# Unit 1's decay sums behind unit 0's state product, in a bank of its own, without zero products: a linear attention and a two-layer network on one core

## The chip, the cores and the metric

The kernel runs on one core of one Trainium2 chip. The metric is the device time of one execution in microseconds (us). The core's engines have these names: PE multiplies matrices (PEld is its loading of weights), DVE is VectorE, ACT is ScalarE, POOL is GpSimd, and SP only issues DMAs. Each engine works through its own list of instructions in order and waits on semaphores for the others.

## The reference

A recurrent attention with a decay for every row of its state, and behind it a network of two layers with a squared relu. B, H, S, D are 4, 8, 768, 48; the width H·D is 384 and the hidden width 2048.

```python
for t in range(S):
    state = alpha[:, :, t, :, None] * state + np.einsum('bhd,bhe->bhde', k[:, :, t], v[:, :, t])
    y[:, :, t] = np.einsum('bhd,bhde->bhe', q[:, :, t], state)
...
x = y.transpose(0, 2, 1, 3).reshape(B * S, H * D)
h = x @ w_in
r = np.maximum(h, 0.0)
out = (r * r) @ w_out
```

## The kernel before

**Units.** The sequence of each of the four batches is cut into three pieces of 256 tokens. A piece of one batch is a unit; units 0 to 3 are the first pieces of the four batches, 4 to 7 the second, 8 to 11 the third. The decays are handled as sums of logarithms within a unit (a product with a triangle of ones), so that a unit needs only products of matrices and one state of the unit before it in its batch.

**Steps of a unit g**, each an operation with a name in the program:

- `lda`, `ldk`, `ldq`, `ldv`: the loads of alpha, k, q and v, 384 KB each. Units 1 to 3 and unit 4's alpha are loaded through GpSimd's queue, in which the pieces of the two weights stand too (`win0` to `win3`, `wout0` to `wout3`); later units through SP's. `lda2` waits for `ldv1`, `ldk1` for `ldk0`.
- Decays: `pr` (product of the alphas of a pair of tokens), `ln` and `lm` (logarithms, on ScalarE), the sums on PE (`m1`, for units 2 and up `m1i`), then the exponentials on ScalarE, `ei`, `ea`, `ec`, and `lb` with `es`, the same for the first token of a pair; `bk` multiplies a part of them.
- `ekm` and `eqm` multiply keys and queries by these. `vc` copies the values to bf16. `tr` transposes keys and queries (on PE up to unit 2, by DMA on SP from unit 3 on) and `et` copies them out of PSUM.
- `p` (scores, on PE; for units 1 and up with the products for the state in the same operation), `mk` (the causal mask), `kv` (unit 0's state product), `sa`, `sc`, `sd` (state at the middle and at the end of the unit), `y` (attention's output), `xe` and `xf` (copies of it), `xt` and `xv` (its transpose).
- The network: `s1_g_u` (first layer, eight pairs of hidden tiles), `re` (relu), `sq` (square), `s2_g_j_s` (second layer, a quarter of the sum each), `oe` (copy out of PSUM), `out` (store).

**Order.** `TABLES` holds one list of these names for each engine, and that is the order in which an engine does them. `add` notes for every operation what it reads and writes, the PSUM banks among them, and `place` sets a wait for another engine only where an operation needs it. So moving a name in a list moves waits too.

**Banks.** `psWH` has three banks: W, H0 and H1. `psO` is one bank: the second layer's sums, and now and then a pair of the first layer. `state_banks` says in which banks a unit's state products stand. For unit 0 these were H0 and H1: H0 is read by `sa0`, H1 by `sc0`. Unit 1's sums `m11` are written to W and H0, so `m11` had to wait for `sa0`. The banks of the sums of units 0 and 1, and those of unit 0's state products:

```python
bank, keys = (psX, [("ps", "X", 0), ("ps", "X", 1)]) if g == 0 else (psWH, [("ps", "W"), ("ps", "H", 0)])
...
return (psH[0][:, 0:HD], psH[1][:, 0:HD]), [("ps", "H", 0), ("ps", "H", 1)]
```

**Zero products.** Entries such as `+512` in PE's list are products of a tile of zeros, 512 or 256 columns wide, which write to `psO` and are read by nobody. They stand only in the first 17 us, between PE's operations of units 0 and 1. Nothing is noted of what they write.

Line numbers below are those of the kernel before: L992 is the first layer, L1038 the second, L1000 and L1002 the relu on ScalarE and VectorE, L1010 and L1014 the square on VectorE and ScalarE, L579 the sums of a later unit, L545 to L551 those of unit 1, L590 and L592 its exponentials `ei` and `ea`, L570 `pr`, L573 `ln`, L614 `lb`, L637 and L636 the copy of the values on ScalarE and GpSimd, L646 `ekm`, L894 the mask, L941 `xv`, L877 the scores, L1086 the zero products, L657 the transposes by DMA.

Of the kernel before, what the change touches and what calls it, by code (L numbers as in the profile page):

```python
# [204 lines left out]

TABLES = {
    "act": """
        table ln0_0 ln1_0 ei0_0 xcaus ea0_0 ei1_0 ea1_0 ec1_0 et00_0 ec0_0 vc0 ln1 et01_0 et11_0 vc1 ei1 ea1 xe0
        ec1 et0_1 re0_0 sa1 re0_1 sq0_1 re0_3 xe1 re0_4 re0_5 lm2 ln2 re0_6 ei2 ea2 ec2 es2 re1_2 re1_3 sq0_6
        re1_4 et0_2 vc2 re1_6 sa2 sq1_6 sq1_3 ln3 lm3 ei3 ea3 ec3 es3 oe0_0 oe0_1 xf2 xe2 lm4 ln4 vc3 ei4 ea4  # L210
        ec4 re2_0 re2_1 es4 oe1_0 re2_2 re2_3 re2_4 ldk5 re2_5 ldq5 sa3 sq2_5 lm5 re2_7 ln5 re2_6 xe3 ei5 ea5
        ec5 xv3 es5 oe2_0 re3_0 oe2_1 lm6 re3_1 xe4 ln6 re3_4 re3_3 ei6 ea6 ec6 re3_6 sq3_5 re3_7 sq3_7 es6
        re4_0 re4_1 re4_2 re4_3 vc6 xe5 lm7 ln7 re4_7 oe3_1 re4_4 ei7 ea7 ec7 re4_6 sq4_6 es7 oe4_0 re5_0 re5_1
        lm8 ln8 xe6 re5_2 re5_3 ei8 ea8 re5_4 re5_5 es8 re5_6 re5_7 sq5_7 re6_0 re6_1 re6_2 oe5_0 vc8 xe7 lm9
        ln9 re6_5 re6_6 oe5_1 re6_7 ei9 ea9 es9 oe6_0 vc9 re7_0 lm10 re7_1 ln10 xe8 re7_3 ei10 ea10 re7_4 re7_5
        es10 re7_6 re7_7 oe7_0 re8_0 re8_1 re8_2 lm11 ln11 xe9 re8_3 re8_4 ei11 ea11 re8_5 re8_6 sq8_5 es11
        sq8_7 re9_0 oe8_0 vc11 re9_1 oe8_1 xe10 re9_3 re9_4 re9_5 re9_6 re9_7 re10_0 oe9_0 re10_1 re10_2 xe11
        oe9_1 re10_3 re10_4 re10_5 re10_6 re10_7 re11_0 oe10_0 re11_1 re11_2 re11_3 oe10_1 re11_4 re11_5 re11_6
        re11_7 oe11_0 oe11_10
    """,  # L220
    "dve": """
        zero zlinc zlstr zident zcaus zcaus1 zla0 zla1 zones zown zown0 zown1 zqk0 zqk1 zqk2 zlb0 zlb1 ekm0_0
        eqm0_0 ekm1_0 eqm1_0 et10_0 mk0_0 sa0 mk1_0 ekm1 eqm0_1 eqm1_1 xv0 et1_1 sc0 mk1_1 mk0_1 sc1 re0_2 xf1
        sq0_3 xv1 pr2 sq0_5 re0_7 re1_0 lb2 re1_1 ekm2 eqm0_2 eqm1_2 sq0_7 re1_5 et1_2 sq1_1 sq1_5 re1_7 mk1_2
        pr3 sc2 mk0_2 lb3 eqm1_3 eqm0_3 ekm3 xv2 pr4 sq1_7 bk4 lb4 ekm4 eqm1_4 eqm0_4 sq2_1 mk1_3 mk0_3 sc3
        oe1_1 sd3 sq2_7 sq2_6 xf3 lb5 ekm5 eqm1_5 eqm0_5 sa4 mk1_4 mk0_4 re3_2 pr6 sc4 sq3_1 xf4 sq3_3 re3_5
        sq3_6 lb6 ekm6 sa5 mk0_5 sc5 mk1_5 eqm0_6 eqm1_6 oe3_0 xf5 sq4_1 re4_5 pr7 sq4_3 sq4_7 sq4_5 bk7 lb7
        eqm0_7 sa6 eqm1_7 ekm7 sc6 sd6 mk0_6 mk1_6 pr8 oe4_1 xf6 sq5_3 bk8 lb8 ekm8 sq5_5 sq5_6 sa7 mk0_7 sc7
        mk1_7 eqm0_8 eqm1_8 sq6_1 re6_3 sd7 sq6_3 pr9 xf7 re6_4 sq6_5 sq6_6 sq6_7 bk9 lb9 ekm9 eqm0_9 eqm1_9
# [4 lines left out]
    """,  # L234
    "pe": """
        +512 +512 +512 +512 +512 +512 +512 +512 m10_0 m11_0 +512 +512 +256 +256 tr00_0 +512 +256 tr10_0 +512
        +256 +256 tr01_0 p0_0 tr11_0 kv0 +512 +512 +512 +256 +256 p1_0 m11 +512 +256 y0 +512 +512 +256 tr0_1 xt0
        tr1_1 s1_0_0 p0_1 s1_0_1 s1_0_3 s1_0_2 s1_0_4 y1 s1_0_5 xt1 s1_0_6 s1_0_7 s1_1_0 m1i2 s1_1_1 s1_1_2
        s1_1_3 s1_1_4 s1_1_5 tr0_2 s1_1_6 tr1_2 s2_0_0_0 s1_1_7 p0_2 s2_0_0_1 s2_0_0_2 s2_0_1_0 s2_0_1_1 m1i3
        s2_0_1_2 s2_0_0_3 s2_0_1_3 y2 s2_1_0_0 s2_1_0_1 xt2 s2_1_0_2 s1_2_0 s1_2_1 m1i4 s2_1_0_3 s1_2_2 s1_2_3  # L240
        s2_1_1_0 s1_2_4 s2_1_1_1 s1_2_5 p0_3 s2_1_1_2 s1_2_6 s1_2_7 s2_1_1_3 y3 m1i5 s2_2_0_0 s2_2_0_1 xt3
        s2_2_0_2 s2_2_0_3 s1_3_0 p0_4 s2_2_1_0 s2_2_1_1 s2_2_1_2 s2_2_1_3 s1_3_2 s1_3_1 y4 s1_3_4 s1_3_3 m1i6
        s1_3_6 s1_3_5 s2_3_0_0 s2_3_0_1 s1_3_7 p0_5 s2_3_0_2 s1_4_0 s1_4_1 s2_3_0_3 s1_4_2 s1_4_3 y5 s2_3_1_0
        s1_4_5 s2_3_1_1 s2_3_1_2 s1_4_7 s2_3_1_3 s1_4_4 m1i7 s2_4_0_0 s1_4_6 s2_4_0_1 s2_4_0_2 p0_6 s2_4_0_3
        s1_5_1 s1_5_0 s2_4_1_0 s2_4_1_1 s1_5_2 s2_4_1_2 s2_4_1_3 y6 s1_5_3 m1i8 s2_5_0_0 s1_5_4 s1_5_5 s2_5_0_1
# [5 lines left out]
        y10 s2_8_1_3 s1_9_3 s1_9_4 s2_9_0_0 s1_9_5 s1_9_6 s2_9_0_1 s1_9_7 p0_11 s2_9_0_2 s1_10_0 s2_9_0_3
        s1_10_1 s1_10_2 s2_9_1_0 s2_9_1_1 y11 s2_9_1_2 s2_9_1_3 s1_10_3 s1_10_4 s2_10_0_0 s1_10_5 s1_10_6
        s2_10_0_1 s1_10_7 s2_10_0_2 s1_11_0 s2_10_0_3 s1_11_1 s1_11_2 s2_10_1_0 s2_10_1_1 s2_10_1_2 s1_11_3
        s2_10_1_3 s1_11_4 s1_11_5 s2_11_0_0 s1_11_6 s1_11_7 s2_11_0_1 s2_11_0_2 s2_11_0_3 s2_11_1_0 s2_11_1_1
# [863 lines left out]
```

## Time and profile before

| | |
|---|---|
| Time, median of 3 runs | 170.76 us (170.74 to 170.88) |
| The profiled execution's own time | 171.26 us |
| Its span, first to last instruction | 169.5 us |
| Granted clock of TensorE | 1.000 |
| Busy: PE, DVE, ACT, POOL | 163.8, 118.0, 109.6, 35.3 us |
| DMA moved | 33.37 MB, 197 GB/s in the mean |

The rows come from one profiled execution, so sums are made against its own time. In a timeline row stand the start and the length in us, the engine, the line, the operation, what it writes and reads, and how many instructions were merged into the row; a bracket tells the idle time ahead of it and what ended it. A length includes the instruction's own tail: the next instruction on an engine often starts before it is over. Landing of a DMA is counted from its issue.

### The profile page before, as it was taken

What the parts mean: (1) busy time and instruction counts of PE and PEld (TensorE: products, weight loads), DVE (VectorE), ACT (ScalarE), POOL (GpSimd) and SP (SyncE); (2) the same over time, 40 slices, a digit from 0 to 9 for tenths busy, and PEclk for the clock granted to TensorE, in tenths of its full rate; (3) what the DMA queues carried; (4) which work ended last, traced back from release to release, by engine and by line L of the source; (5) the groups of instructions that cost most, each with busy time, mean ns of one, the idle gap of its engine ahead of it and who ended that gap; (6) DMA issues with size and microseconds to landing.
All of it is one profiled execution on the core that took longest, in us unless ns stands there. A gap on an engine that the chain in (4) does not pass through costs nothing.

```text
span 169.5 us, 5392 instructions
## 1 busy us (share of the span) xinstructions
PE 163.8 (97%) x2369; PEld 125.9 (74%) x2369; DVE 118.0 (70%) x206; ACT 109.6 (65%) x212; POOL 35.3 (21%) x46
## 2 busy tenths in 40 slices
...
GB/s 137 324 318 188 260 312 215 293 288 252 185 220 329 241 181 197 307 137 243 301 195 247 263 152 258 207 194 288 145 190 205 97 119 58 0 141 4 33 60 93
DMA packets 68407, 33.37 MB, mean 197 GB/s; under 512 B 63520, under 2 KB 65312, under 8 KB 68384
## 3 DMA queue, kind: packets, MB, share of 16 engines
...
q10 hardware_dynamic: 2080, 0.79, 1.8%
...
q14 instruction: 5, 0.04, 0.1%
...
## 4 chain that ended last, share of the span: by engine, by line
PE 83%; DMA 12%; ACT 1%; POOL 1%; issue 1%; DVE 0%; SPq 0%
PE psO L1038 34%; PE psWH L992 33%; DMA raw<-in_alpha_dram 6%; DMA raw<-in_v_dram 3%; DMA raw<-in_k_dram 2%; PE psX L877 2%; PE psZ L765 2%; PE psX L953 2%; PE psWH L1038 2%; PE psWH L730 1%; PE psZ L877 1%; PE psX L765 1%; PE psO L992 1%; PE psWH L579 1%; POOL raw L463 1%; ACT rr L1000 1%
## 5 line engine op out<-in xcount | busy, mean ns | idle before, releaser
L992 PE MATMUL psWH<-xt,win 128*128 128x256 bf16 x552 | 70.5, 273 | 0.9 <-ACT rr L1000 0.9
L1038 PE MATMUL psO<-wout,gt 128*128 128x384 bf16 x352 | 67.0, 326 | 0.0
L992 PEld LDWEIGHTS psWH<-xt,win 128*128 128x128 bf16 x552 | 59.8, 114 | 7.4 <-ACT rr L1000 1.4
L1000 ACT ACTIVATE rr<-psWH 128x512 bf16<-128x512 f32 x79 | 46.5, 599 | 25.3 <-PE psWH L992 24.0
L1038 PEld LDWEIGHTS psO<-wout,gt 128*128 128x128 bf16 x352 | 32.7, 98 | 16.7 <-DVE gt L1010 0.2
L1010 DVE TENSOR_TENSOR gt<-rr 128x1024 bf16<-128x1024 bf16 (+1 forms) x46 | 26.6, 584 | 22.4 <-ACT rr L1000 22.4
L1013 POOL TENSOR_TENSOR gt<-rr 128x1024 bf16<-128x1024 bf16 x3 | 5.7, 1911 | 56.6 <-ACT rr L1000 56.6
L894 DVE TENSOR_TENSOR pm<-psZ,caus 128x1024 bf16<-128x1024 f32 x12 | 14.6, 1216 | 3.7 <-PE psWH L730 3.0
L1045 ACT ACTIVATE osb<-psO 128x384 f32<-128x384 f32 x17 | 8.4, 492 | 11.6 <-PE psO L1038 11.2
L894 DVE TENSOR_TENSOR pm<-psX,caus 128x1024 bf16<-128x1024 f32 x12 | 14.6, 1215 | 0.9 <-PE psX L877 0.5
L641 DVE TENSOR_TENSOR qks<-raw,eq 128x384 bf16<-128x384 f32 x22 | 11.4, 550 | 1.1 <-ACT eq L616 1.0
L646 DVE TENSOR_TENSOR qks<-raw,ek 128x768 bf16<-128x768 f32 x11 | 10.5, 950 | 1.1 <-ACT ek L558 1.0
L1002 DVE TENSOR_SCALAR rr<-psWH 128x512 bf16<-128x512 f32 x13 | 8.8, 683 | 1.2 <-PE psWH L992 1.2
L1014 ACT ACTIVATE gt<-rr 128x512 bf16<-128x512 bf16 (+1 forms) x11 | 8.9, 821 | 0.6 <-DVE rr L1002 0.4
L573 ACT ACTIVATE lab<-prd 128x384 bf16<-128x384 f32 x10 | 5.2, 522 | 6.0 <-DVE prd L570 5.8
L1086 PE MATMUL psO<-zero 128*128 128x512 bf16 (+1 forms) x27 | 7.7, 418 | 1.3 <-DVE zero L382 1.3
L913 DVE CAST xbf<-psZ 128x384 bf16<-128x384 f32 x10 | 5.5, 554 | 3.4 <-PE psZ L757 3.2
L850 POOL TENSOR_TENSOR sbd<-tmp,acm 128x192 bf16<-128x192 f32 x5 | 2.9, 588 | 20.6 <-DVE tmp L840 16.2
L911 ACT ACTIVATE xbf<-psX 128x384 bf16<-128x384 f32 x11 | 5.4, 490 | 2.4 <-PE psZ L757 2.3
L637 ACT ACTIVATE vbf<-raw 128x768 bf16<-128x768 f32 x7 | 5.9, 837 | 1.2 <-DMA raw<-in_v_dram 1.2
L570 DVE TENSOR_TENSOR prd<-raw 128x384 f32<-128x384 f32 x9 | 6.4, 707 | 0.2 <-DMA raw<-in_alpha_dram 0.2
L616 ACT ACTIVATE eq<-la 128x384 f32<-128x384 f32 x10 | 5.2, 522 | 2.0 <-DVE la L614 2.0
...
## 6 DMA issues: line engine op xcount, KB each, us to landing
out_dram<-osb SPq DMA_DIRECT2D x11, 384.0 KB, 3.3
raw<-in_alpha_dram SPq DMA_DIRECT2D x9, 384.0 KB, 5.5
raw<-in_v_dram SPq DMA_DIRECT2D x9, 384.0 KB, 4.4
raw<-in_k_dram SPq DMA_DIRECT2D x8, 384.0 KB, 5.7
raw<-in_q_dram SPq DMA_DIRECT2D x8, 384.0 KB, 4.0
win<-in_moe_w_in_dram POOLq DMA_DIRECT2D x4, 384.0 KB, 8.8
wout<-in_moe_w_out_dram POOLq DMA_DIRECT2D x4, 384.0 KB, 8.9
raw<-in_k_dram POOLq DMA_DIRECT2D x3, 384.0 KB, 6.4
```

The source lines that it names most:

```text
L570: add("dve", lambda e: e.tensor_tensor(hd(PRD[la][:]), al(0), al(1), ALU.mult), dve_ns(HD), p0, reads=[("raw", r, 0)], writes=[("prd", la) ...
L641: add("dve", lambda e, j=j, dst=dst: e.tensor_tensor(dst, RAW[r][:, 2, :, j, :].rearrange("p (n x) d -> p n x d", x=2), EQ[la][:, j].rearr ...
L646: add("dve", lambda e, a=a, E=E: e.tensor_tensor(QKS[qs][:, a, :, :, 0:D], RAW[r][:, 1 + a].rearrange("p h j d -> p j h d"), E[la][:].rear ...
L894: add("dve", lambda e, hf=hf, psT=psT: e.tensor_tensor(PM[pm][:, hf].rearrange("p r n j t -> p (r n) (j t)"), psT[:, :, :].rearrange("p r ...
L992: ins = pe.matmul(psN[:, i * T:(i + 1) * T], WIN[:, kk, hidden(fj)], mov, start=(kk == 0), stop=(kk == KT - 1))
L1000: add("act", lambda e, psN=psN, rr=rr: e.activation(rr, psN, AF.Relu), act_ns(512), pu + 600, reads=[keyN], writes=[("rr", rb, half)], nam ...
L1002: alts={"dve": (lambda e, psN=psN, rr=rr: e.tensor_scalar(rr, psN, 0.0, None, ALU.max), dve_ns(512))})
L1010: add("dve", lambda e, dst=dst, sq=sq: e.tensor_tensor(dst, sq, sq, ALU.mult), 148 + k * 267, pu + 1200, reads=[("rr", rb, h) for h in ran ...
L1014: "act": (lambda e, dst=dst, sq=sq: e.activation(dst, sq, AF.Square), act_ns(k * 512))})
L1038: ins = pe.matmul(psS, GT[gt][:, fj, j, :], WOUT[:, fj, :], start=(fj == 0), stop=(fj == FT - 1))
L1045: add("act", lambda e, j=j, psS=psS: e.activation(OSB[ob][:, j], psS, AF.Copy), act_ns(DM), ps_ + 700, reads=[keyS], writes=[("osb", ob, j ...
L1086: pr.arrange(TABLES, lambda n: lambda pe: pe.matmul(psO[:, 0:n], ZERO[:, 0:128], ZERO[:, 0:n], skip_group_check=True), zero)
```

## The change

Unit 0's state product for the middle of the unit goes to `psO` instead of H0:

```diff
         if g == 0:
-            return (psH[0][:, 0:HD], psH[1][:, 0:HD]), [("ps", "H", 0), ("ps", "H", 1)]
+            return (psO[:, 0:HD], psH[1][:, 0:HD]), [("ps", "O"), ("ps", "H", 1)]
```

In PE's list `m11` moves to the place behind `kv0`, ahead of `p1_0`, and the ten zero products from `kv0` to `tr0_1` go (those ahead of `kv0` stay); `m1i4` moves ahead of `s1_2_0` and `s1_2_1`. The copy of unit 1's values, `vc1`, goes from ScalarE to GpSimd. On ScalarE and VectorE relus, squares and small steps of units 0 to 4 change places, and `sq0_6` goes from ScalarE to VectorE; on SP `out0_1` moves ahead of `ldv4` and of unit 4's transposes. Lines of the lists, each with its start left out:

```diff
  "pe"
-... tr01_0 p0_0 tr11_0 kv0 +512 +512 +512 +256 +256 p1_0 m11 +512 +256 y0 +512 +512 +256 tr0_1 xt0
+... tr01_0 p0_0 tr11_0 kv0 m11 p1_0 y0 tr0_1 xt0
  "act"
-... xe1 re0_4 re0_5 lm2 ln2 re0_6 ei2 ea2 ec2 es2 re1_2 re1_3 sq0_6 re1_4 et0_2 vc2 re1_6 ...
+... xe1 re0_4 re0_5 re0_6 ln2 lm2 ei2 ea2 ec2 es2 re1_2 re1_3 vc2 re1_4 et0_2 re1_6 ...
  "dve"
-... ekm3 xv2 pr4 sq1_7 ...
+... ekm3 pr4 xv2 sq1_7 ...
  "pool"
-... lda2 sd0 ldk2 ldv2 ldq2 ...
+... lda2 vc1 sd0 ldk2 ldv2 ldq2 ...
```

**PE, from unit 0's state product to its output.** This is PE's list of before, from `kv0` (L718) over the second half of unit 0's scores (L877) and unit 1's sums (L545 to L551) to `y0` (L795):

```order
L718 MATMUL psWH<-vbf,qks 128x96 [waits e_act]
L718 MATMUL psWH<-vbf,qks 128x96 x15
L1086 MATMUL psO<-zero 128x512 x3
L1086 MATMUL psO<-zero 128x256 x2
L877 MATMUL psZ<-kqt 64x128 [waits e_act]
L877 MATMUL psZ<-kqt 64x128 x15
L545 MATMUL psWH<-laf,linc 128x384 [waits e_dve]
L546 MATMUL psWH<-laf,linc 128x384
L547 MATMUL psWH<-laf,linc 128x384
L548 MATMUL psWH<-laf,lstr 128x384
L551 MATMUL psWH<-ones,laf 128x2 x8
L1086 MATMUL psO<-zero 128x512
```

And the same place after the change, from the last product of `kv0`:

```order
L718 MATMUL psWH<-vbf,qks 128x96
L545 MATMUL psWH<-laf,linc 128x384 [waits e_act]
L546 MATMUL psWH<-laf,linc 128x384
L547 MATMUL psWH<-laf,linc 128x384
L548 MATMUL psWH<-laf,lstr 128x384
L551 MATMUL psWH<-ones,laf 128x2 x8
L877 MATMUL psZ<-kqt 64x128 [waits e_act]
L877 MATMUL psZ<-kqt 64x128 x15
L795 MATMUL psX<-smd,kqt 64x96 [waits e_dve]
```

The sums stand ahead of the scores now; their wait for VectorE (`sa0`) has become one for ScalarE (unit 1's logarithm), and no zero products follow.

**VectorE, around unit 2's `lb` (L614).** A piece of the difference. The row on `psO` is `re1_1`, the later relu `re1_5`; of the two squares of 512 columns the first is now `sq0_6` and the second `sq0_7`, and L677 copies the transposed keys:

```order
 L1002 TENSOR_SCALAR rr<-psWH 128x512 [waits e_pe] x2
+L1002 TENSOR_SCALAR rr<-psO 128x512 [waits e_pe]
 L614 TENSOR_TENSOR la<-psWH,la 128x384 [waits e_act]
-L1002 TENSOR_SCALAR rr<-psO 128x512 [waits e_pe]
 L646 TENSOR_TENSOR qks<-raw,ek 128x16x48 [waits d_k2pool,e_pool]
 L641 TENSOR_TENSOR qks<-raw,eq 128x4x2x48 [waits d_q2pool,e_act]
 L641 TENSOR_TENSOR qks<-raw,eq 128x4x2x48
+L1002 TENSOR_SCALAR rr<-psWH 128x512 [waits e_pe]
 L1010 TENSOR_TENSOR gt<-rr 128x512
-L1002 TENSOR_SCALAR rr<-psWH 128x512 [waits e_pe]
 L677 COPY kqt<-psZ 128x8x2x64 [waits e_pe]
+L1010 TENSOR_TENSOR gt<-rr 128x512
```

`re1_1` has gone ahead of `lb2`, `re1_5` ahead of the square, and one square of 512 columns has come in.

**PE, at unit 4's sums (L579, L582).** A piece of the difference, between quarters of unit 1's second layer (L1038) and the first pairs of unit 2's first layer (L992):

```order
 L929 MATMUL psX<-ident,xbf 128x2x64 x5
 L1038 MATMUL psO<-wout,gt 128x384 x4
-L992 MATMUL psWH<-xt,win 128x256 [waits e_dve]
-L992 MATMUL psWH<-xt,win 128x256 x11
 L579 MATMUL psWH<-lab,linc 128x384 [waits e_act]
 L582 MATMUL psWH<-ones,lab 128x2 x4
+L992 MATMUL psWH<-xt,win 128x256 [waits e_dve]
+L992 MATMUL psWH<-xt,win 128x256 x11
 L1038 MATMUL psO<-wout,gt 128x384 [waits e_dve]
```

The two pairs `s1_2_0` and `s1_2_1`, twelve products, now come behind the sums `m1i4` instead of ahead of them.

More of the change, by code (lines that the diff above doesn't have):

```diff
@@ L207 @@
     "act": """
[L208 to L217, printed above, removed]
@@ L218 @@
-        oe9_1 re10_3 re10_4 re10_5 re10_6 re10_7 re11_0 oe10_0 re11_1 re11_2 re11_3 oe10_1 re11_4 re11_5 re11_6
-        re11_7 oe11_0 oe11_10
+        table ln0_0 ln1_0 ei0_0 xcaus ea0_0 ei1_0 ea1_0 ec1_0 et00_0 ec0_0 vc0 ln1 et01_0 et11_0 ei1 ea1 ec1 xe0
+        et0_1 re0_0 sa1 re0_1 sq0_1 re0_3 xe1 re0_4 re0_5 re0_6 ln2 lm2 ei2 ea2 ec2 es2 re1_2 re1_3 vc2 re1_4
+        et0_2 re1_6 sa2 sq1_6 sq1_3 ln3 lm3 ei3 ea3 ec3 es3 oe0_0 oe0_1 xf2 xe2 lm4 ln4 vc3 ei4 ea4 ec4 re2_0
+        re2_1 es4 oe1_0 re2_2 re2_3 re2_4 ldk5 re2_5 ldq5 sa3 sq2_5 lm5 re2_7 ln5 re2_6 xe3 ei5 ea5 ec5 xv3 es5
@@ L223 @@
         eqm0_0 ekm1_0 eqm1_0 et10_0 mk0_0 sa0 mk1_0 ekm1 eqm0_1 eqm1_1 xv0 et1_1 sc0 mk1_1 mk0_1 sc1 re0_2 xf1
-        sq0_3 xv1 pr2 sq0_5 re0_7 re1_0 lb2 re1_1 ekm2 eqm0_2 eqm1_2 sq0_7 re1_5 et1_2 sq1_1 sq1_5 re1_7 mk1_2
-        pr3 sc2 mk0_2 lb3 eqm1_3 eqm0_3 ekm3 xv2 pr4 sq1_7 bk4 lb4 ekm4 eqm1_4 eqm0_4 sq2_1 mk1_3 mk0_3 sc3
-        oe1_1 sd3 sq2_7 sq2_6 xf3 lb5 ekm5 eqm1_5 eqm0_5 sa4 mk1_4 mk0_4 re3_2 pr6 sc4 sq3_1 xf4 sq3_3 re3_5
+        sq0_3 xv1 pr2 sq0_5 re0_7 re1_0 re1_1 lb2 ekm2 eqm0_2 eqm1_2 re1_5 sq0_6 et1_2 sq0_7 sq1_1 sq1_5 re1_7
+        mk1_2 pr3 sc2 mk0_2 lb3 eqm1_3 eqm0_3 ekm3 pr4 xv2 sq1_7 bk4 lb4 ekm4 eqm1_4 eqm0_4 sq2_1 mk1_3 mk0_3
+        sc3 oe1_1 sd3 sq2_7 sq2_6 xf3 lb5 ekm5 eqm1_5 eqm0_5 sa4 mk1_4 mk0_4 re3_2 pr6 sc4 sq3_1 xf4 sq3_3 re3_5
         sq3_6 lb6 ekm6 sa5 mk0_5 sc5 mk1_5 eqm0_6 eqm1_6 oe3_0 xf5 sq4_1 re4_5 pr7 sq4_3 sq4_7 sq4_5 bk7 lb7
@@ L236 @@
         +512 +512 +512 +512 +512 +512 +512 +512 m10_0 m11_0 +512 +512 +256 +256 tr00_0 +512 +256 tr10_0 +512
[L237 to L245, printed above, removed]
```

39 lines of the change are left out of this document (28 added, 11 removed).

## The prediction

> **What bounds the kernel now.** The profile's page first, busy time by engine:
>
> ```profile
> PE 163.8 (97%) x2369; PEld 125.9 (74%) x2369; DVE 118.0 (70%) x206; ACT 109.6 (65%) x212; POOL 35.3 (21%) x46
> ```
>
> TensorE (PE) is the bound. Next the windows by stage, to see where it is not full (stretch, its length, PE's busy time and instructions, clock, DMA share, GB/s):
>
> ```profile
> 37.50:45.00 7.50, 6.65 (x91) 1.00 0.90 195
> 45.00:169.00 124.00, 122.16 (x1772) 1.00 0.82 178
> ```
>
> From 45 us on PE lacks 1.84 us, nearly all of it behind its last product; the one large hole lies in 37.5 to 45, 0.85 us. So a gain made early counts only if it is still there at 45. Where PE is held back before that, the chain that ended last tells, in order of time (start, length, what):
>
> ```profile
> 12.47 10.93 DMA raw<-in_alpha_dram
> 23.43 0.57 DVE prd L570
> 24.03 0.53 ACT lab L573
> 24.55 0.49 ACT rr L1000
> 25.09 0.84 PE psO L992 x6
> ...
> 42.25 0.49 ACT ek L590
> ...
> 43.20 0.50 ACT rr L1000
> 43.74 1.50 PE psWH L992 x12
> ```
>
> Two places. Unit 2's alpha lands at 23.40, and its product (pr2), logarithm (ln2) and sums (m1i2, at 24.6) follow; nothing that PE did earlier enters. And unit 4's sums (m1i4) release ScalarE's exponentials ei4 (42.25) and ea4; behind these stands the relu re2_0, which frees the bank that s1_2_2 fills from 43.74.
>
> **The change, part by part: up to 24.6 us.** m11 goes ahead of p1_0, without a wait for sa0, and vc1 leaves ScalarE. The timeline of before (start, length, instruction, idle before it and what ended that):
>
> ```profile
> 12.21 0.84 ACT L637 ACTIVATE vbf<-raw 128x768 bf16<-128x768 f32 x1 [1.18 <-DMA raw<-in_v_dram]
> 12.96 0.79 ACT L558 ACTIVATE ek<-psWH 128x768 f32<-128x768 f32 x1
> 11.55 1.23 DVE L894 TENSOR_TENSOR pm<-psZ,caus 128x1024 bf16<-128x1024 f32 x1 [0.69 <-PE psZ L877]
> 13.78 0.96 DVE L646 TENSOR_TENSOR qks<-raw,ek 128x768 bf16<-128x768 f32 x1 [1.01 <-ACT ek L558]
> 11.43 0.34 PE L545 MATMUL psWH<-laf,linc 128*128 128x384 bf16 x1
> ```
>
> Before, the values' DMA held ScalarE up to 12.21, and ei1 came at 12.96. Now m11 leaves its place behind p1_0 (11.43), and ei1 can start near 11.2. VectorE's ekm1 is then held by mk1_0 alone, which ends at 12.78: 1.0 us sooner than 13.78. y0 and what hangs on it still wait for mk1_0, so I estimate 0.8 of this at the first layer's products. At m1i2 none of it counts: pr2 starts at 23.43 as before, and PE comes early and waits. The start is worth 0; its cover is alpha's DMA, whose issue waits, as before, for unit 1's values.
>
> The copy vc1 stands on GpSimd behind that DMA's issue (12.47) and ahead of sd0 and the next loads. No row shows it there; the nearest is the same copy later (shortest, median, longest ns):
>
> ```profile
> L636 POOL CAST vbf<-raw x4: 819/988/1152, 49.4 to 122.2; 128x768 bf16<-128x768 f32 x4
> ```
>
> Begun by 13.5 it ends by 14.7 at the worst, ahead of ekm1's own end (13.7) plus the transposes and copies for p0_1, which wants it next. ScalarE is rid of 0.84 us. Between a loss of a few tenths, covered by the wait at m1i2, and a gain that the same wait swallows, I take 0.
>
> **The zero products.** Ten go. These rows can price that (zero products as PE starts, then warmed, and the first five of the ten):
>
> ```profile
> 1.25 3.59 PE L1086 MATMUL psO<-zero 128*128 128x512 bf16 x8 [1.25 <-DVE zero L382]
> 5.77 0.81 PE L1086 MATMUL psO<-zero 128*128 128x512 bf16 x4
> 9.82 1.04 PE L1086 MATMUL psO<-zero 128*128 128x512 bf16 x5
> ```
>
> Eight of 512 columns each took 0.43 us apiece; later four of 1,536 columns in all took 0.81 together, with the last one's tail. So PE begins at half rate and doubles after 3.6 (the eight) to 4.5 us of work (1.25 to 5.77). Without the ten it has little to do between p1_0's end (11.4) and the first layer: y0, then transposes. If it falls back to half rate there, the way back costs half of that time, 1.8 to 2.25: I take 2.2 as the upper end (third rival). The other end is 0, as the ten themselves lie where PE would idle. I take 0: before 43.74 PE paused 0.85 us, and the twelve products behind it took their usual 1.50 (40.47, below); the new pause, from 11.43 to y0 at 12.8, is about 1.4 us, nearer to that than to a cold start.
>
> The Trainium skill ("TensorE: Matmul & The Clock Gate", section "What's actually happening") says that the rate falls back after an idle window of about 3.4 us. By that the cost is 0, as taken; no row of before shows a fall. The same page's "Part 4: PE-mode transpose" says that transposes don't count as busy in the same way, which speaks against leaving the zero products out, and would give the third rival's time.
>
> **From 24.6 to 35.5.** Rows of ScalarE, PE and VectorE:
>
> ```profile
> 27.05 1.07 ACT L1000 ACTIVATE rr<-psWH 128x512 bf16<-128x512 f32 x2
> 27.93 0.82 PE L992 MATMUL psWH<-xt,win 128*128 128x256 bf16 x6
> 35.05 0.33 PE L579 MATMUL psWH<-lab,linc 128*128 128x384 bf16 x1
> 26.03 0.56 DVE L614 TENSOR_TENSOR la<-psWH,la 128x384 f32<-128x384 f32 x1 [0.24 <-ACT acm L595]
> 26.51 0.68 DVE L1002 TENSOR_SCALAR rr<-psO 128x512 bf16<-128x512 f32 x1
> 28.91 0.42 DVE L1010 TENSOR_TENSOR gt<-rr 128x512 bf16<-128x512 bf16 x1
> 33.87 0.55 DVE L570 TENSOR_TENSOR prd<-raw 128x384 f32<-128x384 f32 x1
> ```
>
> re0_6 now precedes ln2, so s1_1_1 starts right behind m1i2, near 24.88 instead of 25.09. But re1_1 goes ahead of lb2: it starts when s1_1_1 has ended (24.88 + 0.84, so 25.76), and lb2 0.6 behind it at 26.36, 0.33 late. Behind lb2, es2 and re1_2 on ScalarE slip by as much, re1_2 from 27.05 to 27.38; its bank is s1_1_5's, which starts at 27.97 against 27.93. The 0.2 are gone. Then sq0_6, which ScalarE did, is one more square on VectorE ahead of pr3 (0.42, of which 0.35 to the next start). VectorE is without holes there, so pr3 starts at 34.27 instead of 33.87, and m1i3 behind it at 35.45 instead of 35.05: PE is **0.4 late**.
>
> **From 35.5 to 45.** Rows of PE, ScalarE, VectorE, and of unit 4's alpha (its issue; its time to landing):
>
> ```profile
> 39.66 0.81 PE L1038 MATMUL psO<-wout,gt 128*128 128x384 bf16 x4
> 40.47 1.50 PE L992 MATMUL psWH<-xt,win 128*128 128x256 bf16 x12
> 41.81 0.33 PE L579 MATMUL psWH<-lab,linc 128*128 128x384 bf16 x1
> 41.35 0.83 ACT L637 ACTIVATE vbf<-raw 128x768 bf16<-128x768 f32 x1
> 43.07 1.10 ACT L1000 ACTIVATE rr<-psWH 128x512 bf16<-128x512 f32 x2
> 38.09 0.95 DVE L646 TENSOR_TENSOR qks<-raw,ek 128x768 bf16<-128x768 f32 x1
> 39.86 0.56 DVE L941 COPY xt<-psX 128x768 bf16<-128x768 bf16 x1 [0.82 <-PE psX L929]
> 40.33 0.55 DVE L570 TENSOR_TENSOR prd<-raw 128x384 f32<-128x384 f32 x1
> 28.41 0.91 POOL L463 DMA_DIRECT2D raw<-in_alpha_dram  x1
> raw<-in_alpha_dram POOLq DMA_DIRECT2D x1, 384.0 KB, 9.9
> ```
>
> m1i4 now stands ahead of s1_2_0 and s1_2_1, and pr4 ahead of xv2. Alpha landed at 38.3, so pr4 only waits for its turn: behind ekm3 (now 38.49 to 39.44) it ends by 39.95, and ln4 by 40.5. PE, 0.4 late, reaches m1i4 at 39.66 + 0.4 + 0.65 = 40.7: no wait. The sums are there at 41.1. vc3 runs from 40.4, and the next start on ScalarE can be 0.75 later (12.21 to 12.96), so ei4 at 41.16 instead of 42.25. re2_0 followed it by 0.82 (43.07): now 41.98, its bank free near 42.55. PE meanwhile does m1i4 (0.27), s1_2_0 and s1_2_1 (1.31 at the usual spacing) and s2_1_0_3 (0.65): 40.7 + 2.23 = 42.93. There s1_2_2 starts, without a wait, instead of at 43.74.
>
> **The sum.** Start 0, zero products 0, lateness at m1i3 +0.4, the hole at 43.74 and what stood in it −1.2: together **−0.8**. PE is full behind it, so the gain stays. The profiled execution took 171.26 (span 169.5, 1.76 around it) and would take 170.46; it lies 0.50 above the median of before, 170.76, so the forecast is **169.9**. A measurement tells some 0.2% (0.34 us) from no change. Bounds: without the lateness the bank's 42.55 sets the end, −1.2; with twice the lateness, −0.4.
>
> **The rivals.** *First, the early gain passes m1i2*, should unit 2's alpha land sooner: up to 0.8 more, 169.1. Its unchanged issue speaks against it. Chance 0.06.
>
> *Second, a later wait takes the gain.* On SP out0_1 now goes ahead of ldv4 and of unit 4's transposes, for which p0_4 waits. The transposes' last issue and landing, and p0_4's start in the chain:
>
> ```profile
> L657 SPq DMA_TRANSPOSE kqt<-qks x2: 1325/1902/2478, 45.6 to 48.2; - x2
> DMA to landing us min/median/max: 5.6/5.9/6.3
> 55.98 0.35 PE psX L877 x16
> ```
>
> Landed at 53.8, used at 55.98: 2.2 to spare, 1.4 once PE is 0.8 sooner. 384 KB more ahead cost perhaps 1 us, so it just fits; if they cost 2, some 0.6 of the gain goes: 170.5. Chance 0.19.
>
> *Third, slower: PE falls back to half rate* between 11.4 us and the first layer. For it speaks that little but transposes is left there, against it the pause at 43.74. 2.2 us lost, less the 0.8 that PE would otherwise wait at m1i2, make 1.4 at 24.6, and −0.8 later leaves +0.6: 171.3. It decides from a loss of 1.6 on. Chance 0.25. That the change does not do what it says I leave out: the order shows every move.
>
> **How the numbers follow.** The forecast has 0.50. Faster: 0.48 of it, all of the first rival's 0.06, 0.04 of the second: 0.58. Same: 0.02, 0.12 of the second, 0.05 of the third: 0.19. Slower: 0.03 and 0.20: 0.23. The range goes from 169.4 (between bound −1.2 and the first rival; 0.08 below) to 171.3 (0.12 above). The likeliest case's own range is 169.5 to 170.4.
>
> **What would show it.** Right: m1i2 again near 24.6 with a wait of PE ahead of it; m1i3 near 35.4; m1i4 near 40.7, ahead of s1_2_0; no hole at s1_2_2, and that near 42.9. Wrong: first-layer products of more than the usual spacing between 13 and 20 us; m1i2 later than 24.8; a new wait of PE behind 45 us.

## The result, and the profile after

The changed kernel is slower by about 1%: 173.11 us in the median of 8 executions (171.83 to 175.28) against 170.86 us of the kernel before (170.74 to 171.21), a ratio of 1.0100 with a 95% interval from 1.0070 to 1.0131. The profiled execution took 172.45 us, its span is 170.7 us against 169.5, so this pair of traces shows a loss of 1.2 us. Ratios leave out executions more than 1.5% above the fastest of the same kernel (here two of the eight, 174.55 and 175.28), while medians and ranges hold every execution, so a ratio can be nearer to 1 than the medians are, and number 2 below, with two of six left, has none.

First the page after, busy time by engine. PE has 1.5 us less to do than before, and yet the span is longer:

```profile
PE 162.3 (95%) x2359; PEld 125.8 (74%) x2359; DVE 119.4 (70%) x207; ACT 108.1 (63%) x210; POOL 37.1 (22%) x47
```

Next the windows by stage (stretch, its length, PE's busy time and instructions, clock, DMA share, GB/s), the kernel after:

```profile
24.60:30.00 5.40, 5.07 (x56) 1.00 1.07 221
30.00:37.50 7.50, 7.26 (x113) 1.00 1.01 306
37.50:45.00 7.50, 7.50 (x99) 1.00 0.92 188
45.00:54.00 9.00, 8.63 (x163) 1.00 1.15 259
54.00:58.00 4.00, 2.57 (x78) 1.00 1.08 254
```

and the kernel before in the same places:

```profile
45.00:54.00 9.00, 9.00 (x167) 1.00 1.18 271
54.00:58.00 4.00, 4.00 (x87) 1.00 1.14 306
```

The hole of 0.85 us between 37.5 and 45 is closed, as the prediction said. Behind it PE lacks 1.80 us that it did not lack before, 1.43 of them at one place. PE's timeline after, at the prediction's steps (start, length, instruction, idle before it and what ended that): unit 2's sums m1i2, unit 3's m1i3, unit 4's m1i4, then s1_2_2, then unit 4's scores p0_4:

```profile
24.53 0.33 PE L579 MATMUL psWH<-lab,linc 128*128 128x384 bf16 x1
35.39 0.34 PE L579 MATMUL psWH<-lab,linc 128*128 128x384 bf16 x1 [0.24 <-ACT lab L573]
40.66 0.33 PE L579 MATMUL psWH<-lab,linc 128*128 128x384 bf16 x1
42.89 0.82 PE L992 MATMUL psWH<-xt,win 128*128 128x256 bf16 x6
57.08 0.42 PE L877 MATMUL psX<-kqt 64*64 64x128 bf16 x16 [1.43 <-issue]
```

p0_4 in PE's timeline of before (the prediction's chain row has 55.98 for the same products):

```profile
55.91 0.42 PE L877 MATMUL psX<-kqt 64*64 64x128 bf16 x16
```

s1_2_2 starts at 42.89, 0.85 sooner than the 43.74 of before (the forecast was 0.81), and p0_4 comes 1.2 later than before. Here the gain went, and more. What p0_4 waits for is unit 4's second transpose. Its issues and landings after, to be read beside the same rows of before in the prediction:

```profile
L657 SPq DMA_TRANSPOSE kqt<-qks x2: 1432/2962/4491, 45.3 to 49.8; - x2
DMA to landing us min/median/max: 7.2/8.4/9.5
```

The first was issued at 45.25 and landed 9.5 later; the second went out at 49.8 and landed 7.2 later, at 57.0. Before it landed at 53.8, from an issue at 48.2. So of the 3.2 us by which the second lands later, one half, 1.6, is its later issue, behind a first issue that held SP longer, and the other half, 1.6, its longer flight. SP's list after shows where they stand (a start, the time for which the issue held SP):

```profile
42.87 1.18 SPq L463 DMA_DIRECT2D raw<-in_alpha_dram  x1
44.10 0.63 SPq L1054 DMA_DIRECT2D out_dram<-osb  x1
44.78 0.43 SPq L463 DMA_DIRECT2D raw<-in_v_dram  x1
45.25 5.96 SPq L657 DMA_TRANSPOSE kqt<-qks  x2
```

out0_1 (L1054), which stood behind them at 49.52 before, goes ahead, and the first transpose's issue alone held SP 4.5 us (2.5 before). The chain of waits points to another place:

```profile
47.02 7.73 DMA raw<-in_q_dram
54.75 0.02 issue
54.77 1.04 DVE qks L641 x2
55.81 1.27 issue
57.08 0.42 PE psX L877 x16
```

This is unit 5's q and its product on VectorE, done at 55.81. p0_4 doesn't read them, and the 1.27 us of "issue" behind them are the rest of the wait for the transpose. The row is useful for something else: the same q load took 5.0 us before and 7.7 now. The other plain transfers issued between 42 and 50 us were slower too: 5.8 to 7.2 us to landing, 5.1 to 5.7 before.

### The profile page after: what moved, and what is told of

The parts are those of the page before. It is cut to its first block, busy times and chain, and to the rows that moved or that the text cites. A ratio compares the mean times of both kernels' runs of the same rounds, so it can differ in the third digit from the quotient of the medians.

```text
span 170.7 us, 5373 instructions
## 1 busy us (share of the span) xinstructions
PE 162.3 (95%) x2359; PEld 125.8 (74%) x2359; DVE 119.4 (70%) x207; ACT 108.1 (63%) x210; POOL 37.1 (22%) x47
## 4 chain that ended last, share of the span: by engine, by line
PE 77%; DMA 13%; DVE 3%; POOL 3%; issue 2%; ACT 1%; SPq 0%
PE psWH L992 32%; PE psO L1038 31%; DMA win<-in_moe_w_in_dram 6%; DMA raw<-in_q_dram 5%; DMA raw<-in_k_dram 2%; PE psZ L765 2%; PE psX L877 2%; POOL raw L463 2%; PE psX L953 2%; PE psX L765 1%; PE psWH L730 1%; PE psZ L877 1%; PE psWH L579 1%; POOL win L434 1%; PE psO L992 1%
## 5 line engine op out<-in xcount | busy, mean ns | idle before, releaser
L992 PE MATMUL psWH<-xt,win 128*128 128x256 bf16 x552 | 70.6, 273 | 0.5 <-ACT rr L1000 0.3
L1038 PE MATMUL psO<-wout,gt 128*128 128x384 bf16 x352 | 67.0, 326 | 0.0
L992 PEld LDWEIGHTS psWH<-xt,win 128*128 128x128 bf16 x552 | 59.7, 114 | 6.7 <-ACT rr L1000 0.8
L1038 PEld LDWEIGHTS psO<-wout,gt 128*128 128x128 bf16 x352 | 32.8, 98 | 16.6 <-DVE gt L1010 0.2
L1010 DVE TENSOR_TENSOR gt<-rr 128x1024 bf16<-128x1024 bf16 (+1 forms) x47 | 27.6, 594 | 22.4 <-ACT rr L1000 22.3
L1045 ACT ACTIVATE osb<-psO 128x384 f32<-128x384 f32 x17 | 8.3, 490 | 13.1 <-PE psO L1038 12.7
L641 DVE TENSOR_TENSOR qks<-raw,eq 128x384 bf16<-128x384 f32 x22 | 12.0, 580 | 1.4 <-ACT eq L616 1.0
L1014 ACT ACTIVATE gt<-rr 128x1024 bf16<-128x1024 bf16 (+1 forms) x10 | 8.3, 840 | 0.6 <-DVE rr L1002 0.4
L1086 PE MATMUL psO<-zero 128*128 128x512 bf16 (+1 forms) x17 | 5.5, 466 | 1.3 <-DVE zero L382 1.3
L877 PE MATMUL psX<-kqt 64*64 64x128 bf16 x192 | 5.0, 222 | 1.7 <-issue 1.4
L877 PEld LDWEIGHTS psX<-kqt 64*64 64x64 bf16 x192 | 3.1, 106 | 4.4 <-issue 3.5
```

The source lines that it names most:

```text
L641: add("dve", lambda e, j=j, dst=dst: e.tensor_tensor(dst, RAW[r][:, 2, :, j, :].rearrange("p (n x) d -> p n x d", x=2), EQ[la][:, j].rearr ...
L877: ins = pe.matmul(psT[64 * c:64 * c + 64, rr_, o:o + 128], keys, mov)
L992: ins = pe.matmul(psN[:, i * T:(i + 1) * T], WIN[:, kk, hidden(fj)], mov, start=(kk == 0), stop=(kk == KT - 1))
L1010: add("dve", lambda e, dst=dst, sq=sq: e.tensor_tensor(dst, sq, sq, ALU.mult), 148 + k * 267, pu + 1200, reads=[("rr", rb, h) for h in ran ...
L1014: "act": (lambda e, dst=dst, sq=sq: e.activation(dst, sq, AF.Square), act_ns(k * 512))})
L1038: ins = pe.matmul(psS, GT[gt][:, fj, j, :], WOUT[:, fj, :], start=(fj == 0), stop=(fj == FT - 1))
```

## The experiments

Each was compared with the kernel before on the same chip, where that one's median was 170.85 to 170.98 us. Some edits add lines to the kernel, so that line numbers in the rows of those runs are up to four higher (L659 is L657, L879 is L877). "p0_4" is its start in the profiled execution, with PE's wait ahead of it; "osb" is PE's wait, a little later, for a free output buffer.

| | median us (range; executions) | ratio, 95% interval | span | p0_4 (wait) | osb |
|---|---|---|---|---|---|
| 1 change, store back | 171.58 (170.74–174.52; 11) | 1.0046 [1.0019, 1.0072] | 172.8 | 58.67 (1.09) | 0.44 |
| 2 before, store ahead | 174.27 (170.76–175.30; 6) | no ratio | 170.8 | 57.22 (1.78) | – |
| 3 before, sums sooner | 170.27 (169.65–174.48; 12) | 0.9958 [0.9939, 0.9978] | 168.4 | 54.17 | 0.60 |
| 4 before, start alone | 171.24 (170.76–171.87; 12) | 1.0022 [1.0005, 1.0038] | 169.3 | 55.67 | – |
| 5 the same, zero products kept | 171.10 (170.76–172.28; 12) | 1.0009 [0.9988, 1.0030] | 169.0 | 55.41 | – |
| 6 change, zero products kept | 174.48 (172.87–175.10; 6) | 1.0180 [1.0136, 1.0225] | 173.4 | 58.08 (2.75) | – |
| 7 sums sooner, loads later | 171.21 (170.83–172.03; 12) | 1.0012 [0.9993, 1.0031] | 169.6 | 54.70 | 1.12 |
| 8 sums sooner, values earlier | 171.69 (169.65–172.07; 12) | 1.0010 [0.9977, 1.0044] | 169.7 | 54.64 | 1.35 |
| 9 change, store back, zero products kept | 170.49 (170.05–171.87; 12) | 0.9982 [0.9959, 1.0004] | 168.5 | 54.85 | – |
| 10 as 3, third output buffer | 170.25 (169.59–172.32; 12) | 0.9949 [0.9927, 0.9971] | 169.2 | 55.60 (1.22) | – |
| 11 as 7, third output buffer | 169.83 (169.52–170.30; 6) | 0.9930 [0.9908, 0.9952] | 168.2 | 54.17 | – |
| 12 as 9, third output buffer | 170.29 (169.88–171.38; 12) | 0.9961 [0.9943, 0.9979] | 168.5 | 54.88 | – |
| 13 as 9, store early on ScalarE's queue | 171.87 (171.37–172.67; 12) | 1.0053 [1.0034, 1.0073] | 170.1 | 56.52 (1.05) | – |
| 14 as 6, zero products in the pause | 173.66 (172.58–174.27; 6) | 1.0144 [1.0111, 1.0176] | 171.7 | 58.05 (1.35) | – |
| 15 as 12, loads later | 170.46 (169.76–171.76; 12) | 0.9958 [0.9932, 0.9983] | 170.0 | 56.38 | – |

The table holds a regularity. Before, p0_4 starts at 55.91 in PE's timeline and the span is 169.5: 113.6 us lie between. After it is 170.7 − 57.08, again 113.6. With the osb wait added to p0_4's start the difference is 113.6 to 113.8 in all but two of the 15 rows: number 6 (115.3), whose clock falls, and number 11 (114.0), for whose extra 0.4 us I have found no single cause. So what the change does is decided by the time at which PE gets through p0_4 and the next osb wait, and by the clock behind them.

### The store's place: numbers 1 and 2

Number 1 undoes one move in the changed kernel, number 2 makes it alone in the kernel before. A piece of SP's list in number 2:

```diff
-lda5 ldv4 tr0_4 tr1_4 out0_1 ldv5
+lda5 out0_1 ldv4 tr0_4 tr1_4 ldv5
```

> The changed kernel with out0_1 back behind unit 4's transposes on SP, all else changed. Theory (the store ahead of the transposes is what holds p0_4 back from 55.1 to 57.1): tr1_4 lands near 53.5, p0_4 starts near 55.1 without a wait, and the 0.85 us won at s1_2_2 stays: 170.0 us, 0.5% faster than before. Rival (PE being 0.85 us earlier, with ScalarE's loads of unit 5 issued 0.9 earlier, collides with the transposes whatever the store does): p0_4 still waits 1 us or more, 171.0 us or above.

> The kernel before with one edit: on SP out0_1 ahead of ldv4 and of unit 4's transposes. Theory: tr1_4 lands near 56.5 to 57.5 instead of 53.8, p0_4 waits 0.5 to 1.5 us beyond 55.98, 171.4 to 172.4 us. Rival (only together with an earlier PE): tr1_4 lands by 56, 170.7 to 171.1 us.

The store ahead, alone, makes the kernel before slower by 3.4 us in the median. Four of its six executions took 173.7 to 175.3, the other two 172.57 and 170.76. The profiled one is that of 172.57: the transposes, issued from 45.1, landed late, the second at 57.1 as expected, and p0_4 waited, a little longer than the 0.5 to 1.5 us expected. Landings, then PE's timeline, of number 2:

```profile
DMA to landing us min/median/max: 8.2/9.0/9.8
```

```profile
57.22 0.42 PE L877 MATMUL psX<-kqt 64*64 64x128 bf16 x16 [1.78 <-issue]
```

PE's work was not moved at all here, so in this trace the store's place suffices for the wait. Number 1 got back 1.5 us of the medians' 2.25, though not the sums' gain: 171.58 instead of the 170.0 expected. Its profiled execution, the slowest of its eleven, shows another part of the loss at its largest (number 4 below has a milder case). The windows of number 1:

```profile
14.00:15.00 1.00, 0.81 (x14) 1.00 1.19 181
15.00:16.00 1.00, 0.39 (x6) 0.54 1.22 192
16.00:18.00 2.00, 2.00 (x14) 0.50 1.25 207
18.00:20.00 2.00, 2.00 (x68) 0.50 1.23 234
20.00:22.00 2.00, 2.00 (x12) 0.52 1.06 332
22.00:24.00 2.00, 2.00 (x54) 1.00 1.06 310
```

The granted clock fell to half for some 6.8 us behind the place where the zero products had stood, and m1i2 came at 27.02 instead of 24.53. That is the prediction's third rival, seen on the chip, though not in every execution. p0_4 still waited 1.09 in this trace, with transposes that took 9.4 and 7.5 us, as number 1's own rival had said; number 9 below, in which the clock holds, shows no such wait.

### The sums and the start, one at a time: numbers 3, 4 and 5

Number 3 makes only the two moves that bring unit 4's sums forward, number 4 only the start (the state product in `psO`, m11 ahead, no zero products, vc1 on GpSimd), number 5 the start with nine zero products kept (the six marked `!` also wait for sa0, since psO now holds the state). Pieces of the lists:

```diff
-s2_1_0_2 s1_2_0 s1_2_1 m1i4 s2_1_0_3        # 3, PE
+s2_1_0_2 m1i4 s1_2_0 s1_2_1 s2_1_0_3
-ekm3 xv2 pr4                                # 3, VectorE
+ekm3 pr4 xv2
-kv0 m11 p1_0 y0 tr0_1                       # 5 against 4, PE
+kv0 m11 p1_0 !512 !512 !512 !512 !512 !256 y0 +512 +512 +256 tr0_1
```

> The kernel before with two edits: m1i4 ahead of s1_2_0 and s1_2_1 on PE, pr4 ahead of xv2 on VectorE. Theory (these two close the hole at 43.74; the rest of the change only adds 0.4 us of lateness at m1i3): m1i3 at 35.05, m1i4 near 40.3, s1_2_2 near 42.6, 1.1 us sooner, and 169.8 us, 0.6% faster. Rival (an earlier PE alone collides with the DMAs of units 4 and 5): p0_4 waits, 170.5 us or above.

> The kernel before with the start of the change alone: unit 0's state in psO, m11 ahead of p1_0, no zero products from kv0 on, vc1 on GpSimd. Theory (the early gain is swallowed by the wait for unit 2's alpha): s1_0_0 0.6 us sooner, m1i2 within 0.1 us of 24.6, 170.6 to 171.0 us, no change. Rival (the missing zero products or the copy on GpSimd cost time): m1i2 later than 24.9, 171.2 us or above.

> The start of the change alone (as in the run of the start alone) with zero products put back: five of 512 and one of 256 columns behind p1_0, waiting for sa0, and the former three behind y0. Theory (without them PE falls to half rate in some executions, and that is all that the start costs): granted clock 1.00 throughout, m1i2 near 24.4, 170.7 to 171.0 us, no change. Rival (the copy on GpSimd or the new order costs the 0.4 us): 171.2 us again, with the clock at 1.00.

The sums alone are a gain, 0.9958, a little less than expected (170.27 for 169.8); three of the twelve executions took 172.3 to 174.5, and no trace shows what held them. In the profiled execution p0_4 starts 1.74 sooner than before (54.17 for 55.91); 0.5 of that belongs to this execution, for m1i3, ahead of the edit, stood at 34.53 instead of 35.05 already. The span falls by 1.1 only. The rest is a second wait. PE's timeline of number 3:

```profile
54.17 0.42 PE L877 MATMUL psX<-kqt 64*64 64x128 bf16 x16
55.66 2.77 PE L1038 MATMUL psO<-wout,gt 128*128 128x384 bf16 x16 [0.60 <-ACT osb L1045]
```

The copy of unit 2's output (oe2_0, L1045) writes the output buffer that unit 0 used, and there are two of them; so it waits until out0_1 has landed, here 49.25 + 5.8 = 55.05, and PE waits for the bank. Before, the store landed at 54.9 and the copy ran at 55.36: the slack was under half a microsecond. The start alone is worth nothing or a little less (1.0022, 171.24 us, at the rival's 171.2). With zero products 1.0009; these two intervals overlap. Number 4's profiled execution shows the fall of the clock again, shorter (windows of number 4), while in number 5 all these windows stand at 1.00:

```profile
13.00:14.00 1.00, 1.00 (x41) 0.68 1.25 200
14.00:15.00 1.00, 1.00 (x11) 0.50 1.15 161
15.00:16.00 1.00, 1.00 (x12) 0.50 1.17 181
16.00:18.00 2.00, 2.00 (x74) 0.81 1.24 205
```

It still reached m1i2 at 24.38, without a wait ahead of it: the fall, 3.3 us, was over by 17 us, and its first layer had begun at 16.03, still ahead of the 16.41 of before. In number 1, where the fall lasted longer, the lateness stayed. The mean clock points the same way: 0.99 in nine of number 4's twelve executions (171.03 to 171.87 us) and 1.00 in three (170.76 to 171.08), 1.00 in all twelve of number 5.

### Zero products and store crossed: numbers 6 and 9

> The changed kernel with the same zero products put back, the store still ahead of unit 4's transposes. Theory (two losses in the changed kernel, the clock's fall and the transposes' late landing, and the second is the larger): clock 1.00, p0_4 still waits 1 us or more, 171.8 to 173 us. Rival (the clock's fall is most of it): 170.4 us or less.

> The changed kernel with out0_1 back behind tr1_4 on SyncE's queue, and with the zero products kept in a bank of their own. It leaves out of the change the moved store and the removal of the zero products. If these two are what costs: no half rate at 15 to 22 us, p0_4 waits under 0.3 us, and what is left is the sums' 0.85 us less the wait for out0_1 to land ahead of oe2_0 (0.5 us or so): 170.3, between 170.0 and 170.8. Rival, that the sooner sums crowd the transfers whatever the store's place: p0_4 waits 1 us, 171.3.

Number 9 came out as expected, number 6 slower than either expectation. With the zero products kept, the store's place is worth 174.48 against 170.49; the two intervals lie far apart. With the store back, the zero products are worth 171.58 (number 1) against 170.49, 1.0046 against 0.9982, intervals apart too. So both are shown as costs. Keeping the zero products does not help while the store is ahead; number 6 is slower than the change itself. Its windows behind p0_4 tell why:

```profile
57.00:58.00 1.00, 0.00 (x0) 1.00 1.21 312
58.00:59.00 1.00, 0.92 (x65) 0.99 1.17 324
59.00:60.00 1.00, 1.00 (x4) 0.50 1.17 324
60.00:61.00 1.00, 1.00 (x5) 0.50 1.17 323
61.00:62.00 1.00, 1.00 (x4) 0.50 3.06 283
62.00:63.00 1.00, 1.00 (x6) 0.81 0.05 5
```

The pause ahead of p0_4 was 2.75 us (the second transpose landed at 58.0), and from 59 us on PE ran at half its clock for over 3 us.

### Is it the pause that brings the clock down? Number 14

Eight more zero products of 512 columns, into a bank that is free then, stand ahead of p0_4 and run while it waits (a piece of PE's list):

```diff
-s1_3_0 p0_4 s2_2_1_0
+s1_3_0 ?512 ?512 ?512 ?512 ?512 ?512 ?512 ?512 p0_4 s2_2_1_0
```

> The changed kernel with the zero products kept (174.5, its profile at half clock from 58.5 to 62 us behind a pause of 2.75 us), with eight more zero products of 512 columns (1.7 us at the full clock) ahead of p0_4, which run while it waits. If the pause brings the half clock: none after it, and 172.5 to 173.3, the fast end of the runs without them. If the clock falls for another reason, or the pause is only part of it: 174.5 again, half rate at 58 to 62 us. They can lengthen the path by as much as they overrun the wait, at most 1.7 us.

p0_4 starts where it did in number 6, 58.05, and PE's idle time ahead of it is 1.35 instead of 2.75. Windows of number 14:

```profile
57.00:58.00 1.00, 0.00 (x0) 1.00 1.17 316
58.00:59.00 1.00, 0.95 (x65) 1.00 0.78 171
59.00:60.00 1.00, 1.00 (x7) 1.00 1.06 293
60.00:61.00 1.00, 1.00 (x9) 1.00 1.36 187
```

The clock stays, and the span is 171.7 instead of 173.4 from the same start of p0_4: 1.7 us were the half clock in these two traces. The mean clock over the whole span was 1.00 in all six executions, 0.99 in four of six in number 6. The median, 173.66, lies above the 172.5 to 173.3 expected and 0.8 below number 6's, and the two ratios' intervals overlap from 1.0136 to 1.0176; the traces and the clocks, not these medians, carry the point. In the changed kernel's own trace the pause was 1.43, and the clock beyond it stayed at 1.00; that its executions of 174 to 175 us had this fall, or the one at the start, is argued from their lower mean clock (0.98 and 0.99), not seen in a trace.

### The store's 384 KB, or its place in SP's queue? Number 13

The store is issued by ScalarE at 42.95 us: earlier than in the change (44.10), but not in SP's queue. A piece of ScalarE's list; the line that issues the store also names ScalarE for unit 0:

```diff
-es4 oe1_0 re2_2                             # ScalarE; out0_1 leaves SP's list
+es4 oe1_0 out0_1 re2_2
```

> The changed kernel with the zero products kept (170.5 with the store behind the transposes on SyncE, 174.5 with it ahead), with out0_1 issued by ScalarE behind oe1_0, about 43.9 us, as early as in the changed kernel but not on SyncE's queue. If the store's 384 KB on the DMA engines are what holds the transposes: they land at 55 to 57 us, p0_4 waits 1 us or more, 172 to 174.5. If its place in SyncE's queue is what holds them: the transposes land at 52 to 54 us, p0_4 does not wait, 170.2 to 170.8.

Landings, then PE's timeline, of number 13; in number 9, the same kernel with the store behind the transposes, the first landed in 7.8 and the second in 5.7:

```profile
L659 SPq DMA_TRANSPOSE kqt<-qks x2: 3096/3380/3663, 45.4 to 49.1; - x2
DMA to landing us min/median/max: 7.3/8.0/8.7
```

```profile
56.52 0.42 PE L879 MATMUL psX<-kqt 64*64 64x128 bf16 x16 [1.05 <-issue]
```

The second transpose was issued at 49.1 instead of 47.3 and took 7.3 instead of 5.7: the store's bytes in flight hold back the transposes, and their issue, from another queue as well. This run costs 1.4 us over number 9, the store in SP's queue 4.0 (number 6), of which 1.7 in its trace are the clock. Of the expectation by bytes, the landing (56.4) and the wait came true and the time just missed (171.87 for 172 or more); the other one failed. So the bytes are a cause by themselves, and the place in SP's queue, or the issue 1.3 us later there (44.25 in number 6), adds to it; the two were not told apart.

### Does moving transfers help? Numbers 7 and 8

Number 7 delays unit 5's k and q loads on ScalarE's queue, number 8 puts unit 4's values ahead of unit 3's transposes; both on number 3. Pieces of the lists:

```diff
-re2_4 ldk5 re2_5 ldq5 sa3 sq2_5             # 7, ScalarE
+re2_4 re2_5 sa3 ldk5 sq2_5 ldq5
-ldk4 ldq4 tr0_3 tr1_3 lda5 ldv4 tr0_4       # 8, SP
+ldk4 ldq4 ldv4 tr0_3 tr1_3 lda5 tr0_4
```

> The kernel before with m1i4 and pr4 moved ahead, and ScalarE's loads ldk5 and ldq5 each about 1 to 1.5 us later (behind sa3 and behind sq2_5). Theory (unit 4's transposes share the 16 DMA engines with these two loads): tr0_4 lands within 6.5 us of its issue, no executions above 171 us, median 169.7. Rival (what delays the transposes is what stands in SP's own queue ahead of them): tr0_4 again 8 us or more, some executions at 172 to 174.5.

> The kernel before with m1i4 and pr4 moved ahead, and ldv4 on SP ahead of unit 3's transposes instead of between lda5 and unit 4's. Theory (the loads that stand in SP's own queue ahead of unit 4's transposes delay them): tr0_4 is issued in under 2 us and lands within 6 us, no executions above 171 us, median 169.7. Rival (the loads on ScalarE's queue delay them): as with m1i4 and pr4 alone, 170.2 with some executions at 172 to 174.5.

In both, the first transpose of unit 4 lands sooner than number 3's 8.2 (6.0 and 6.9), and in the profiled executions p0_4 does not wait, as it did not in number 3; yet neither gains, against an expected 169.7. Number 7, 171.21, loses what the sums had won. Number 8's executions fall into two groups, four at 169.65 to 170.24 and eight at 171.48 to 172.07, and its profiled one is of the second. The store now lands at 56.1 and 56.3 (6.4 from its issue in both), and the osb wait is 1.12 and 1.35: in these traces what was taken off one transfer fell on another. PE's timeline of number 7:

```profile
56.71 2.77 PE L1038 MATMUL psO<-wout,gt 128*128 128x384 bf16 x16 [1.12 <-ACT osb L1045]
```

### A third output buffer: numbers 10, 11, 12 and 15

```diff
-NRAW, NQKS, NKQT, NPM, NV, NXT, NGT, NRR, NOSB = 4, 3, 3, 2, 4, 4, 3, 4, 2
+NRAW, NQKS, NKQT, NPM, NV, NXT, NGT, NRR, NOSB = 4, 3, 3, 2, 4, 4, 3, 4, 3
```

> The sums alone (the sums' order and pr4 ahead of xv2) with three output buffers instead of two, so that oe2_0 no longer waits for the landing of out0_1. If that landing is what ends the sums' gain: psO L1038 of unit 2 has no wait on osb, the span falls by the 0.6 us that it took there, 169.6 (169.4 to 169.9). Rival, that something else stands right behind it (p0_4's transposes had 1 us to spare, the next loads likewise): 170.2, as with the sums alone.

> The sums with unit 5's k and q loads later on ScalarE's queue, and three output buffers. With two buffers this stood at 171.2 with an osb wait of 1.1 us. If that wait was the whole of it: 170.1 less nothing else, 169.9 to 170.3. Rival, that the later loads themselves are missed by unit 5's chain: still 171 and a wait at unit 5's first products (p0_5 or its transposes).

> The changed kernel with the store back, the zero products kept and three output buffers. If the store ahead of the transposes, the clock at the start and the two output buffers are the three things that took the sums' gain: 169.7 (169.5 to 170.1), PE at the full clock throughout, no wait at p0_4 over 0.2 us nor on osb. Rival, that the transfers of 42 to 57 us are late for PE in another place: 170.3 or more.

> The changed kernel with its store back, the zero products kept, three output buffers, and unit 5's k and q loads later on ScalarE's queue. If the loads crowd the transposes and the store and nothing else is left: 169.7 (169.4 to 170.0), with no execution above 170.6. Rival, that the start's own costs (the products that wait for ScalarE at 24 to 30 us) are what is left: 170.2, as with the loads early.

The osb wait is gone in all four. On the sums alone that brings no more (170.25 after 170.27; 169.6 was expected): in number 10's trace the transposes are the next in line, at 7.4 and 8.3. PE's timeline of number 10:

```profile
55.60 0.42 PE L877 MATMUL psX<-kqt 64*64 64x128 bf16 x16 [1.22 <-issue]
```

With the loads later as well, number 11, both are out of the way. Landings, then PE's timeline, of number 11:

```profile
DMA to landing us min/median/max: 5.6/5.7/5.8
```

```profile
54.17 0.42 PE L877 MATMUL psX<-kqt 64*64 64x128 bf16 x16
54.99 2.77 PE L1038 MATMUL psO<-wout,gt 128*128 128x384 bf16 x16
```

It is the best version of this study, 169.83 (169.9 to 170.3 was expected), 0.7% faster than the kernel before (0.5% to 0.9%); the sums alone gave 0.4%. Added to them by itself, the buffer gave nothing more that these intervals show, and the later loads lost (number 7, whose interval lies above number 3's). Number 12 brings the whole change, without its store in front and with the zero products, to 0.9961; its trace has neither wait and the full clock, but 170.29 misses the 169.5 to 170.1 expected. Number 15 was expected at 169.7 and came to 170.46: a miss. Its profiled execution, its slowest, starts late: a piece of the first weight landed at 17.8, a product of the first layer waited 1.67 us for it and began at 17.89 (the first of that layer in number 12: 16.21), and p0_4, without a wait, came 1.5 later than in number 12. Whether the later loads add nothing to number 12 or this start hides it stays open.

## Why the prediction was wrong, point by point

**The start, 0.** Right in time: m1i2 came at 24.53 (24.61 before), and number 5 agrees, 1.0009. Its cover was not the one named. The trace shows no wait of PE ahead of m1i2, which was to be a sign of being right. The first layer began 0.66 sooner (15.75 for 16.41, forecast 0.8), and nothing of that was left at 21.50 (21.42 before). Only numbers 9 and 14, with the zero products, show the wait, 0.25 and 0.29. Nor is 24.6 fixed: six kernels with the start of before (2, 3, 7, 8, 10, 11) reach m1i2 between 24.02 and 24.45.

**Zero products, 0.** The size was wrong. What was given a chance as the third rival happens in some executions: half clock for 3.3 us (number 4) and 6.8 us (number 1) behind 13 us, 1.1 us in the medians of numbers 1 and 9. The rival's own upper end, 2.2 us lost and 1.4 of lateness at m1i2, was too small: half a clock over 6.8 us costs 3.4, and m1i2 was 2.5 late in number 1's trace. The argument for 0, a pause of only 1.4 us ahead of y0, does not decide it either: the pause was 1.33 in number 4, with the fall, and 1.33 in the changed kernel's trace, without it.

**From 24.6 to 45.** Right, each within 0.1: s1_1_5 behind a wait of 0.33 (27.92), m1i3 at 35.39 (forecast 35.45), m1i4 at 40.66 (40.7), s1_2_2 at 42.89 (42.93), window 37.5 to 45 full. The lateness of 0.4 is there as well: from m1i2 to m1i3 it took 10.86 instead of 10.44.

**"PE is full behind it, so the gain stays."** This is the step that failed. PE was full behind 45 us because two transfers landed just ahead of their use: the second transpose with 2.2 us to spare, and the store of unit 0, which frees the output buffer, with under half a microsecond. The first I had seen, but put into the second rival and at nothing in the sum; of the two it alone binds in the changed kernel's trace, whose wait behind 45 us is the prediction's own last sign of being wrong. The second was not in the prediction, and came out in numbers 1, 3, 7 and 8.

**The second rival's size.** The store ahead was to cost the transposes "perhaps 1 us", at worst 2. The second landed at 57.0 instead of 53.8: 3.2. Put into the rival's own sum, 1.4 to spare and 3.2 of cost make a wait of 1.8 and, less the gain of 0.8, a loss of 1.0; the pair of traces shows 1.2. The mechanism was right, its price was a guess that no row carried. What a pause at that place can do to the clock (number 6) was in no rival. The medians lie 2.25 apart; what the changed kernel loses beyond its trace is not seen in any.

**The gain itself.** The sums were to bring −1.2 without the lateness, −0.8 with it. The sizes were right where no transfer stood in the way. From m1i2 to p0_4 it took 31.30 us before, 30.07 in number 11 (−1.23) and 30.50 in number 12, which has the lateness (−0.80). In the medians that is −1.13 (number 11 against before) and −0.67 (number 12).

**The clock.** A pause of 2.75 us was followed by half rate (number 6); one of 1.43 and one of 1.78 were not (the change and number 2). At the start a thin stretch was enough: in number 1 the clock fell at 15.1 us, when PE had been busy for 0.35, 0.32, 0.55 and 0.81 of the four microseconds ahead, and in number 4 at 13.35, behind 0.39 and 0.28; in the changed kernel's trace 0.48 and 0.19 at the same place were followed by no fall. By the Trainium skill's page "TensorE: Matmul & The Clock Gate" (section "What's actually happening"), an idle window of about 3.4 us is what brings the rate down. As a bound on a single pause that figure is too generous in this kernel.
